# Attention with a hashed mask and two gated mixers on one core: the first pair of heads is read from one buffer and prepared by three engines

## The chip, the cores and the metric

The program runs on 1 core of a Trainium2 chip. The metric is device time in microseconds of one execution, as the median of several. Before the change it is 559.13 us (three runs, 557.96 to 561.72).

## What is computed

The reference has three stages: attention under a mask made from hashes, then two gated mixers on its output. The changed code belongs to the first stage alone.

```
def _attn_ref(q, k, v, proj):                     # 2 batches, 8 heads, 768 rows, 64 columns
    q_bits = (q @ proj > 0); k_bits = (k @ proj > 0)          # 6 bits for each row
    mask = q_bucket[:, :, :, None] == k_bucket[:, :, None, :]
    scores = np.where(mask, scale * q @ k^T, -1e9)
    attn = softmax(scores)
    return attn @ v
x = moe(attn)        # k = relu(xk @ w_k); sigmoid(xr @ w_r) * (k*k @ w_v)
return moe2(x)       # two projections, normalised rows, a product over the sequence
```

All values are float32. The kernel gets that accuracy on TensorE from rounded values: a number is split into a rounded part and a low part (x minus the rounded part), and products of both are summed.

## The kernel before

**Tiling.** Heads come in 8 pairs (`pp`). A pair has two heads, `e` = 0 and 1. Its queries are cut into two halves of 384, and each half gives six units: for each head three blocks (`j`) of 128 queries against all 768 keys. So there are 96 units. The loop `for p in range(np3)` handles three units in each of its 32 iterations, p = 0 to 31.

**A unit.** `scores` (L326) makes 128 x 768 scores in PSUM with four matmuls over 128 rows. The operand of a head is `tk` (`TK[pp % 2][e]`, 128 x 4 x 768): slots 0 and 3 are the rounded k and q, slot 1 holds the low part of k in one half of the rows and the hash bits of k in the other, and slot 2 the rounded q and the hash bits of q. Thus the mask is part of the same matmuls, with bits scaled by 2^30. `peak` (L336, VectorE) copies the scores out of PSUM and takes each row's maximum, `bias` (L344, VectorE) scales it, `expo` (L354, ScalarE) takes the exponential and the sum, `move` transposes six blocks on TensorE (L364) and copies them to `PT` (L370, ScalarE), and `av` (L399, TensorE) multiplies by v. The first `av` comes in iteration 3, for the units of iterations 0 and 1. Buffers limit how far engines run apart: `s` has two, `p` three, `t` (PSUM) three, `PT` two.

**Preparing a pair.** `load_x` fetches x, the pair's k and q (768 KB). `load_pair` fetches the same rows again with four transfers of POOL's queue that round on the way, straight into slots 0 and 2 of one half of the rows and slots 0 and 3 of the other. `split_part` or `split_piece` subtracts to get the low parts. `bits_mm` (L275) multiplies x with the hash vectors, `bits_sign` (L282) and `bits_scale` (L289) make scaled bits of them, and `bits_place` puts eight strips of 12 x 384 into the two `tk`. For the first pair all this stands ahead of the loop: two strips each on VectorE (L303) and ScalarE (L305), four by SP's queue (L307). `clear` (L311) sets the rows beside the bits to zero.

**Warming.** `warm(n)` issues n matmuls of the identity (L267), whose results nobody reads: 12 at the very start, 8 behind the first bits.

**The order of the work.** The order is written out by hand. Each engine does its instructions in program order. The dictionary `plan` keeps further work at slots (p, k): k = 0 behind the second exponential of iteration p, k = 1 at its end. Under it stand the next pair's loads and splits, and the weights of the later stages, 512 x 128 in a unit (`weight_jobs`): a load by SP's queue, `magnitude` on ScalarE (L41), `clamp` (L44), `shift` (L49), `top` (L55), `power` (L62), `low` (L65) on VectorE, `first` on ScalarE (L71), `rest` on POOL (L76, L77). `plan_unit` puts the steps of a unit around an iteration `p0`, by one of the tables `late`, `soon` and `first`.

## Time and profile before

| what | value |
|---|---|
| median of three runs | 559.13 us |
| the profiled execution's own time | 557.71 us |
| its span, from the first to the last instruction | 555.9 us |
| busy TensorE | 543.1 us (98%) |
| busy VectorE, ScalarE, POOL | 370.6, 335.6, 144.6 us |
| mean granted TensorE clock | 0.997 |
| chain that ended last, by engine | PE 86%, DVE 7%, ACT 5%, issue 1%, DMA 1% |

PE is TensorE, DVE is VectorE, ACT is ScalarE, SP is the engine whose queue issues most loads. The profiled execution was 1.42 us faster than the median, and 1.81 us of its time lie outside the span.

### The profile page before, as it was taken

The page shows a single profiled execution, that of the slowest core. Times are in us where ns is not written, and L with a number is a line of the kernel's source. Part 1 is how long each engine was busy: PE and PEld are TensorE (multiplying, and loading weights), DVE is VectorE, ACT ScalarE, POOL GpSimd, SP SyncE. Part 2 cuts the span into 40 slices and gives each one's busy share as a digit, 9 for nine tenths or more (in the row PEclk, how much of TensorE's full clock was granted, in tenths as well). Part 3 has the DMA queues.
Part 4 walks back from the last instruction along what each step waited for, and adds up shares of the span by engine and source line. Part 5 has one row for each costly group of instructions (what it writes and reads, how often), then busy time and mean ns, then how long its engine had stood idle before and what let it go on. Part 6 is the DMA issues. An engine that isn't in the chain of part 4 may idle for free.

```text
span 555.9 us, 9001 instructions
## 1 busy us (share of the span) xinstructions
PE 543.1 (98%) x3188; PEld 466.4 (84%) x3188; DVE 370.6 (67%) x812; ACT 335.6 (60%) x718; POOL 144.6 (26%) x152
## 2 busy tenths in 40 slices
PE   7899999999999999999999999999999999999997
PEld 6766767676767677689999999999998999899896
DVE  6688787877877779458796775316997784443230
ACT  1888888888888889749843856429345343221211
POOL 5684948485857533200000000000110000000000
PEclk9899999999999999999999999999999999999999
DMA  8949494949595710210031211000572100001102
GB/s 175 270 142 177 127 190 125 194 135 181 143 173 168 151 49 16 72 71 26 15 113 39 73 42 39 0 1 8 191 228 85 58 29 1 2 19 39 57 20 95
DMA packets 20478, 51.96 MB, mean 93 GB/s; under 512 B 3841, under 2 KB 6865, under 8 KB 20433
## 3 DMA queue, kind: packets, MB, share of 16 engines
q1 hardware_dynamic: 13664, 31.44, 18.4%
q0 software_dynamic: 6336, 19.66, 17.7%
q8 instruction: 25, 0.41, 0.3%
q10 hardware_dynamic: 432, 0.28, 0.2%
q14 instruction: 21, 0.16, 0.1%
HBM read 47.08 MB, written 3.19 MB: 90 GB/s over the span
## 4 chain that ended last, share of the span: by engine, by line
PE 86%; DVE 7%; ACT 5%; issue 1%; DMA 1%; ACTq 0%; DVEq 0%; POOLq 0%
PE s L326 11%; PE o L399 11%; PE t L364 11%; PE o L176 11%; PE v L638 9%; PE k L176 8%; PE s L176 7%; PE w L176 5%; PE u L176 5%; PE o L638 3%; PE r L176 3%; DVE p L336 2%; DMA tk<-in_kq_dram 1%; ACT tk L121 1%; ACT p L354 1%
## 5 line engine op out<-in xcount | busy, mean ns | idle before, releaser
L336 DVE TENSOR_SCALAR_CACHE_REDUCE p<-s 128x768 f32<-128x768 f32 x96 | 91.8, 956 | 29.4 <-PE s L326 27.9
L354 ACT ACTIVATE p<-p,nb 128x768 f32<-128x768 f32 x96 | 90.5, 943 | 14.0 <-DVE nb L344 13.2
L370 ACT COPY PT<-t 128x384 f32<-128x384 f32 x192 | 83.6, 477 | 19.9 <-PE t L364 18.8
L326 PE MATMUL s<-tk 128*128 128x384 f32 x384 | 85.0, 355 | 3.8 <-DVE p L336 2.1
L326 PEld LDWEIGHTS s<-tk 128*128 128x128 f32 x384 | 64.6, 190 | 23.1 <-DVE rt L382 6.6
L364 PE MATMUL t<-ident,p 128*128 128x128 f32 x576 | 80.4, 280 | 3.4 <-ACT p L354 1.7
L364 PEld LDWEIGHTS t<-ident,p 128*128 128x128 f32 x576 | 65.5, 142 | 14.6 <-ACT PT L370 5.0
L399 PE MATMUL o<-PT,v 128*64 128x384 f32 x384 | 68.8, 494 | 0.0
L258 POOL TENSOR_TENSOR tk<-x,tk 64x384 fp32r<-64x384 f32 x56 | 59.1, 1086 | 2.5 <-issue 1.6
L176 PE MATMUL k<-tk,wk 128*128 128x384 f32 x336 | 59.6, 334 | 0.0
L176 PEld LDWEIGHTS k<-tk,wk 128*128 128x128 f32 x336 | 58.4, 188 | 0.0
L638 PE MATMUL v<-k,wv 128*128 128x384 f32 x288 | 53.6, 334 | 0.0
L638 PEld LDWEIGHTS v<-k,wv 128*128 128x128 f32 x288 | 50.3, 188 | 0.0
L399 PEld LDWEIGHTS o<-PT,v 128*64 128x64 f32 x384 | 24.8, 136 | 28.5 <-issue 26.5
L697 POOL DMA_DIRECT2D wsp<-in_w_spT_dram x6 | 3.6, 612 | 167.8 <-DVE w_a L44 161.3
L176 PE MATMUL o<-wk,tk 128*128 128x512 f32 (+1 forms) x168 | 36.2, 374 | 0.0
L176 PEld LDWEIGHTS o<-wk,tk 128*128 128x128 f32 x168 | 30.0, 188 | 5.5
L619 ACT ACTIVATE kr<-k 128x384 f32<-128x384 f32 x28 | 13.6, 487 | 31.2 <-PE k L176 31.0
L176 PE MATMUL r<-tk,wr 128*128 128x384 f32 x168 | 30.9, 338 | 0.2 <-DVE tk L122 0.2
L121 ACT CAST tk<-g 128x384 fp32r<-128x384 f32 x16 | 8.2, 514 | 37.5 <-DVE g L768 37.5
L176 PE MATMUL w<-wk,tk 128*128 128x512 f32 x132 | 30.7, 390 | 0.0
L176 PEld LDWEIGHTS r<-tk,wr 128*128 128x128 f32 x168 | 29.1, 188 | 1.9 <-ACT PT L370 0.6
(108 smaller groups left out, 851.1 us busy)
## 6 DMA issues: line engine op xcount, KB each, us to landing
tk<-in_kq_dram POOLq DMA_DIRECT2D x32, 384.0 KB, 9.7
x<-in_kq_dram POOLq DMA_DIRECT2D x6, 768.0 KB, 5.6
w_raw<-in_w_k_dram SPq DMA_DIRECT2D x8, 512.0 KB
w_raw<-in_w_v_dram SPq DMA_DIRECT2D x8, 512.0 KB
w_raw<-in_w_in_dram SPq DMA_DIRECT2D x8, 512.0 KB
v<-in_vP_dram SPq DMA_DIRECT2D x8, 384.0 KB
rb<-ds SPq DMA_DIRECT2D x32, 96.0 KB
out_dram<-ot SPq DMA_DIRECT2D x11, 256.0 KB
```

What stands on the lines that cost most here:

```text
L121: nc.scalar.copy(hi, src)
L176: nc.tensor.matmul(o, a, x, start=(i == 0), stop=(i == len(seq) - 1))
L258: nc.gpsimd.tensor_sub(tk[l, 1 + 2 * t, o], raw[pp][l, t, o], tk[l, 2 * t, o])
L326: nc.tensor.matmul(s[:, c, :HS], w, t[:, n, c * HS:(c + 1) * HS], start=(n == 0), stop=(n == 1),)
L336: nc.vector.tensor_scalar(c, s[:, :, :HS], -BIG / 2, None, op0=ALU.max, op1=ALU.max, accum_out=m)
L354: nc.scalar.activation(c, c, AF.Exp, bias=nb, scale=0.125, accum_out=den[g][:, u:u + 1])
L364: nc.tensor.transpose(t[:, 128 * n:128 * n + 128], p[:, k0:k0 + 128], ident)
L370: nc.scalar.copy(PT[g][:, e, 3 * c:3 * c + 3, 128 * j:128 * j + 128], t[:, :HS].rearrange("p (n q) -> p n q", n=3),)
L399: nc.tensor.matmul(obank[64 * e:64 * e + 64, :HS], vt[g // 2][:, kt, e, :], PT[g][:, e, kt, :], start=(kt == 0), stop=(kt == 5),)
L619: nc.scalar.activation(r, o[:, :HS], AF.Relu)
L638: nc.tensor.matmul(os[m][:, :HS], w, x, start=(c == 0 and k == 0), stop=(c == 7 and k == 2),)
L697: nc.gpsimd.dma_start(wsp[c // 3][:, 0, c % 3, :], w_spT[128 * c:128 * c + 128, :])
```

## The change

The first pair is prepared in another way, the second pair's loads and the first weights are moved ahead, and one evacuation is moved.

- Loads at the start: x of the first pair comes in two transfers, k first and then q, into a `PT` buffer (`load_halves`). SP's queue then fetches x of the second pair (its buffer `x` is free for that), the first weight unit and v. POOL's queue fetches only head 1's `tk` (two transfers in place of four).
- Head 0's `tk` is made from x by copies: on VectorE (k, one half of the rows), ScalarE (k, the other half; q) and POOL (half of q). The subtractions are on VectorE (k of both heads) and POOL (q, in halves, `first_low`).
- Bits: `bits_mm` runs twice, the second time with the hash vectors shifted by 12 columns (`msc` gets two columns for that), so that each head's strips lie on rows where an engine can take them. `place` scales and writes a strip in one instruction: two on VectorE, four on ScalarE, two on POOL. `bits_scale` and the four transfers of L307 are gone for this pair.
- `make_identity` moves to the start, `warm` gets 7 and 3 matmuls in place of 12 and 8, and the 3 stand behind the scores of units 0 and 1. Zero fills are shared by VectorE and POOL, all four at the start.
- POOL issues the second pair's four transfers in the middle of the first pair's preparation, behind a subtraction that needs head 1's data.
- The subtraction of head 1's k (VectorE) moves into slot (0, 0).
- The first weight unit follows a new table `start`: `magnitude` in (0, 1), `clamp` and `shift` in (1, 0), `top` in (2, 0), `first` and `power` in (2, 1), one iteration or half of one earlier than by `first`.
- The last evacuation of iteration 0 is VectorE's.

```diff
-WARM_A, WARM_B = 12, 8
+WARM_A, WARM_B = 7, 3
+        def load_halves(pp):
+            b, p = divmod(pp, NP)
+            raw[pp] = mid.tile([128, 2, S], F32, tag="PT", bufs=2, name="x")
+            for t in range(2):
+                nc.sync.dma_start(raw[pp][:, t, :], kq[b, p, t])
...
+        def place(zb, e, g, eng):
+            dst, src, by = place_at(0, e, g), zb[32 * g:32 * g + 12, :], cst_sb[32 * g:32 * g + 12, 1:2]
+            if eng is nc.scalar:
+                nc.scalar.mul(dst, src, by)
+            else:
+                eng.tensor_scalar(dst, src, by, None, op0=ALU.mult)
+
+        def first_low(e, n):
+            l, o = lo_rows[e], slice(n * HS, n * HS + HS)
+            t = TK[0][e]
+            nc.gpsimd.tensor_sub(t[l, 3, o], raw[0][l, 1, o], t[l, 2, o])
+
+        def first_pair():
+            x, t = raw[0], TK[0][0]
+            lo, hi = lo_rows[0], hi_rows[0]
+            h0, h1 = slice(0, HS), slice(HS, S)
+            nc.vector.tensor_copy(t[lo, 0, :], x[lo, 0])
+            nc.scalar.copy(t[hi, 0, :], x[lo, 0])
+            nc.vector.tensor_sub(t[lo, 1, :], x[lo, 0], t[lo, 0, :])
+            nc.scalar.copy(t[lo, 2, h0], x[lo, 1, h0])
+            nc.scalar.copy(t[hi, 3, h0], x[lo, 1, h0])
+            nc.scalar.copy(t[lo, 2, h1], x[lo, 1, h1])
+            first_low(0, 0)
+            nc.gpsimd.tensor_copy(t[hi, 3, h1], x[lo, 1, h1])
+            bits_mm(0)
+            bits_sign(0)
+            z0 = zs.pop(0)
+            place(z0, 0, 2, nc.vector)
+            place(z0, 0, 3, nc.scalar)
+            place(z0, 0, 0, nc.vector)
+            bits_mm(0, 12)
+            bits_sign(0, "zc")
+            z1 = zs.pop(0)
+            for g in (2, 3, 0):
+                place(z1, 1, g, nc.scalar)
+            first_low(1, 0)
+            load_pair(1)
+            first_low(0, 1)
+            place(z0, 0, 1, nc.gpsimd)
+            place(z1, 1, 1, nc.gpsimd)
+            first_low(1, 1)
...
+        start = ((-2, 1), (-1, 0), (-1, 0), (0, 0), (0, 1), (0, 1), (1, 0), (1, 0))
...
-            plan_unit(2 + 2 * n, late if n % 2 else soon if n else first, ld, jobs)
+            plan_unit(2 + 2 * n, late if n % 2 else soon if n else start, ld, jobs)
...
         nc.scalar.dma_start(msc, misc)
-        nc.vector.memset(ident, 0.0)
-        load_x(0)
-        load_pair(0)
-        clear(0, nc.vector)
+        load_halves(0)
+        make_identity(nc, ident)
+        load_pair(0, (1,))
+        clear(0, 0, nc.vector)
+        clear(1, 0, nc.vector)
+        clear(0, 1, nc.gpsimd)
+        clear(1, 1, nc.gpsimd)
+        load_x(1)
+        for job in plan.pop((-1, 1)):
+            job()
+        load_v(0)
         warm(WARM_A)
-        split_part(0, 0, 1, nc.gpsimd)
-        split_part(0, 0, 0, nc.vector)
-        bits_mm(0)
-        bits_sign(0)
-        bits_scale(0, nc.vector)
-        bits_place(0, True)
-        warm(WARM_B)
+        first_pair()
         for r in rcs:
             nc.vector.memset(r, 0.0)
-        split_part(0, 1, 0, nc.vector)
-        split_part(0, 1, 1, nc.gpsimd)
-        make_identity(nc, ident)
-        load_v(0)
+        plan.setdefault((0, 0), []).insert(0, lambda: split_part(0, 1, 0, nc.vector))
...
-            move(a + 1, 1)
+            move(a + 1, 1, nc.scalar.copy if p else nc.vector.tensor_copy)
```

VectorE at the start of the program, before the change, from its first instruction to the first unit's maximum (`tk_0_77` is head 0's operand, `tk_1_78` head 1's):

```order
L489 MEMSET ident 128x128
L311 MEMSET tk_0_77 64x1536
L311 MEMSET tk_1_78 64x1536
L263 TENSOR_TENSOR tk_0_77<-x,tk_0_77 64x768
L282 TENSOR_SCALAR zb<-z,msc 128x384
L289 TENSOR_SCALAR zc<-zb,msc 128x384
L303 CAST tk_0_77<-zc 12x384 x2
L502 MEMSET rc_89 128x32
L502 MEMSET rc_90 128x32
L263 TENSOR_TENSOR tk_1_78<-x,tk_1_78 64x768
L336 TENSOR_SCALAR p,m<-s 128x768
```

The same stretch of VectorE in the change, from behind its two zero fills (the maximum of a unit is L379 there):

```order
L327 CAST tk_0_77<-x 64x768
L329 TENSOR_TENSOR tk_0_77<-x,tk_0_77 64x768
L288 TENSOR_SCALAR zb<-z,msc 128x384
L316 TENSOR_SCALAR tk_0_77<-zb,msc 12x384 x2
L288 TENSOR_SCALAR zb<-z,msc 128x384
L548 MEMSET rc_89 128x32
L548 MEMSET rc_90 128x32
L379 TENSOR_SCALAR p,m<-s 128x768
L387 TENSOR_SCALAR nb<-m 128x1
L379 TENSOR_SCALAR p,m<-s 128x768
L387 TENSOR_SCALAR nb<-m 128x1
L269 TENSOR_TENSOR tk_1_78<-x,tk_1_78 64x768
```

Head 1's subtraction (last row) went from ahead of the first maximum to behind the second one, the separate scaling is gone, and a copy and a second sign have come in.

POOL at the start of the program in the change, from its first transfers on (`tk_0_87` and `tk_1_88` are the second pair's operands):

```order
L252 DMA tk_1_78<-in_kq_dram 64x2x768
L253 DMA tk_1_78<-in_kq_dram 64x2x768
L354 MEMSET tk_1_78 64x1536
L354 MEMSET tk_1_88 64x1536
L321 TENSOR_TENSOR tk_0_77<-x,tk_0_77 64x384
L334 CAST tk_0_77<-x 64x384
L321 TENSOR_TENSOR tk_1_78<-x,tk_1_78 64x384
L252 DMA tk_0_87<-in_kq_dram 64x2x768
L253 DMA tk_0_87<-in_kq_dram 64x2x768
L252 DMA tk_1_88<-in_kq_dram 64x2x768
L253 DMA tk_1_88<-in_kq_dram 64x2x768
L321 TENSOR_TENSOR tk_0_77<-x,tk_0_77 64x384
```

Before, POOL issued four transfers for the first pair, did two subtractions of 64 x 768, made the identity and filled with zeros, and only then issued the second pair's four; now these stand behind the third of its short operations, and two strips and another subtraction follow them.

VectorE in iteration 2, before the change, from the second maximum to the third:

```order
L336 TENSOR_SCALAR p,m<-s 128x768
L344 TENSOR_SCALAR nb<-m 128x1
L379 TENSOR_SCALAR rc_89<-den 128x6
L380 RECIPROCAL rc_89<-rc_89 128x6
L382 STREAM_TRANSPOSE rt<-rc_89 128x32
L44 TENSOR_SCALAR w_a<-w_a 128x512
L49 TENSOR_SCALAR w_a<-w_a 128x512
L336 TENSOR_SCALAR p,m<-s 128x768
```

In the change these two weight steps stand one iteration earlier, ahead of the second pair's sign:

```order
L379 TENSOR_SCALAR p,m<-s 128x768
L387 TENSOR_SCALAR nb<-m 128x1
L44 TENSOR_SCALAR w_a<-w_a 128x512
L49 TENSOR_SCALAR w_a<-w_a 128x512
L288 TENSOR_SCALAR zb<-z,msc 128x384
L379 TENSOR_SCALAR p,m<-s 128x768
```

Behind the reciprocals of iteration 2 stands `top` (L55) alone.

## Rows read from the trace of the kernel before

**Rows 1.** Busy time by stretch (start:end length, PE, PEld, DVE, ACT, POOL, clock, DMA share, GB/s)

```profile
0.00:33.40 33.40, 26.67 (x156) 21.91 (x157) 23.50 (x50) 17.84 (x39) 22.11 (x30) 0.95 0.87 192
33.40:330.00 296.60, 294.38 (x1836) 233.54 (x1836) 228.83 (x535) 232.51 (x507) 118.81 (x117) 1.00 0.46 113
```

**Rows 2.** Chain that ended last, 0 to 40 us (start us, us, what)

```profile
1.24 6.28 DMA tk<-in_kq_dram
...
8.53 0.63 DVE zb L282
...
9.19 1.21 DVE zc L289
...
10.42 0.35 DVE tk L303
...
11.24 2.57 DVE tk L263
13.81 0.89 DVE p L336 x2
...
14.91 1.04 ACT p L354 x2
...
28.39 0.76 DVE w_a L44
...
29.16 1.10 DVE w_a L49
...
33.41 2.09 PE o L399 x12
```

**Rows 3.** Timeline of VectorE and POOL at the first subtractions (start us, us, engine line op)

```profile
7.55 0.95 DVE L263 TENSOR_TENSOR tk<-x,tk 64x768 fp32r<-64x768 f32 x1 [3.25 <-DMA tk<-in_kq_dram]
7.60 2.57 POOL L263 TENSOR_TENSOR tk<-x,tk 64x768 fp32r<-64x768 f32 x1 [3.79 <-DMA tk<-in_kq_dram]
...
11.18 1.83 POOL L263 TENSOR_TENSOR tk<-x,tk 64x768 fp32r<-64x768 f32 x1 [1.01 <-DVE tk L303]
```

**Rows 4.** Timeline of TensorE up to the first scores

```profile
1.05 5.39 PE L267 MATMUL o<-ident 128*128 128x128 f32 x24 [1.05 <-DVE ident L489]
...
6.38 0.85 PE L275 MATMUL z<-x,msc 128*32 128x384 f32 x8
...
7.16 2.05 PE L267 MATMUL o<-ident 128*128 128x128 f32 x16
```

**Rows 5.** Timeline of ScalarE, 10 to 33 us (in brackets idle time before, and its releaser)

```profile
10.42 1.03 ACT L305 CAST tk<-zc 12x384 fp32r<-12x384 f32 x2 [7.92 <-DVE zc L289]
...
18.61 0.85 ACT L370 COPY PT<-t 128x384 f32<-128x384 f32 x2
21.01 0.48 ACT L370 COPY PT<-t 128x384 f32<-128x384 f32 x1 [1.55 <-PE t L364]
...
31.42 0.94 ACT L354 ACTIVATE p<-p,nb 128x768 f32<-128x768 f32 x1 [1.37 <-DVE nb L344]
```

**Rows 6.** Busy time in single microseconds (columns as in rows 1)

```profile
13.00:14.00 1.00, 0.00 (x0) 0.00 (x0) 1.00 (x2) 0.00 (x0) 0.93 (x5) 1.00 0.09 18
...
18.00:19.00 1.00, 1.00 (x5) 1.00 (x4) 0.00 (x0) 1.00 (x4) 1.00 (x3) 0.50 1.04 412
```

**Rows 7.** DMA queue of SP from 4 to 5 us (packets, MB, share of 16 engines)

```profile
q1 hardware_dynamic: 84, 0.21, 52.3%
```

**Rows 8.** Transfers of POOL's line L246, from issue to landing

```profile
DMA to landing us min/median/max: 6.3/9.3/11.3
```

**Rows 9.** Groups by line and form, 0 to 200 us (count, busy us, mean ns, idle us before)

```profile
L336 DVE TENSOR_SCALAR_CACHE_REDUCE p<-s 128x768 f32<-128x768 f32 x83 | 79.4, 956 | 26.8 <-PE s L326 25.3 <-ACT p L354 1.2
...
L258 POOL TENSOR_TENSOR tk<-x,tk 64x384 fp32r<-64x384 f32 x56 | 59.1, 1086 | 2.5 <-issue 1.6
L246 POOL DMA_DIRECT2D tk<-in_kq_dram x16 | 10.0, 626 | 0.8 <-POOLq L871 0.8
L311 POOL MEMSET tk<- 64x1536 f32 x2 | 2.7, 1374 | 0.1
```

More of the change, by code (lines that the diff above doesn't have):

```diff
@@ L109, in hash_attention_moe_kernel @@
     ident = per.tile([128, 128], F32, name="ident")
-    msc = per.tile([128, 42], F32, name="msc")
+    msc = per.tile([128, 44], F32, name="msc")
     pb, cst_sb = msc[:, 0:32], msc[:, 32:34]
@@ L239, in load_x, with load_pair @@
             (nc.gpsimd if pp > 1 else nc.sync).dma_start(raw[pp], kq[b, p].rearrange("t r s -> r t s"))
-        def load_pair(pp):
+        def load_halves(pp):
             b, p = divmod(pp, NP)
-            for e in range(2):
+            raw[pp] = mid.tile([128, 2, S], F32, tag="PT", bufs=2, name="x")
+            for t in range(2):
+                nc.sync.dma_start(raw[pp][:, t, :], kq[b, p, t])
+        def load_pair(pp, es=(0, 1)):
+            b, p = divmod(pp, NP)
+            for e in es:
                 src = kq[b, p][:, 64 * (1 - e):64 * (1 - e) + 64].rearrange("t d s -> d t s")
@@ L269, in attention, with bits_mm @@
         zs = {}
-        def bits_mm(pp):
+        def bits_mm(pp, c0=0):
             zs[pp] = ps_t.tile([128, 512], F32, tag="t", name="z")
@@ L275, in bits_mm, with bits_sign @@
                 nc.tensor.matmul(
-                    zs[pp][32 * g:32 * g + 32, :HS], pb, raw[pp][:, 1 - g // 2, o:o + HS],
-                    start=True, stop=True,
-                )
-        def bits_sign(pp):
-            zb = at.tile([128, HS], F32, tag="zb", name="zb")
+                    zs[pp][32 * g:32 * g + 32, :HS], msc[:, c0:c0 + 32],
+                    raw[pp][:, 1 - g // 2, o:o + HS], start=True, stop=True,
+                )
+        def bits_sign(pp, tag="zb"):
+            zb = at.tile([128, HS], F32, tag=tag, name="zb")
             nc.vector.tensor_scalar(
@@ L290, in bits_scale, with place_at, bits_place @@
             zs[pp] = zc
-        def bits_place(pp, first=False):
+        def place_at(pp, e, g):
+            o = (g % 2) * HS
+            return TK[pp % 2][e][64 * e:64 * e + 12, 2 - g // 2, o:o + HS]
+        def bits_place(pp):
             zc = zs.pop(pp)
@@ L295, in bits_place @@
                 for g in range(4):
-                    o = (g % 2) * HS
-                    a0 = 64 * e
                     s0 = 32 * g + 12 * e
-                    dst = TK[pp % 2][e][a0:a0 + 12, 2 - g // 2, o:o + HS]
-                    src = zc[s0:s0 + 12, :].bitcast(F32)
-                    if first and e == 0:
-                        if g % 2:
-                            nc.vector.tensor_copy(dst, src)
-                        else:
-                            nc.scalar.copy(dst, src)
-                    else:
-                        nc.sync.dma_start(dst.bitcast(F32), src)
@@ L309, in clear @@
-        def clear(r, eng):
-            for e in range(2):
-                eng.memset(TK[r][e][hi_rows[e], 1:3, :].bitcast(F32), 0.0)
+                    nc.sync.dma_start(
+                        place_at(pp, e, g).bitcast(F32), zc[s0:s0 + 12, :].bitcast(F32)
+                    )
+        def place(zb, e, g, eng):
[4 more added lines that the diff above has]
+                eng.tensor_scalar(dst, src, by, None, op0=ALU.mult)
@@ L313, in attention, with clear @@
+        def clear(r, e, eng):
+            eng.memset(TK[r][e][hi_rows[e], 1:3, :].bitcast(F32), 0.0)
         nunits = npairs * 12
@@ L365, in transp, with evac @@
             return t
-        def evac(i, c, t):
+        def evac(i, c, t, copy=nc.scalar.copy):
             g, u = divmod(i, 6)
             e, j = divmod(u, 3)
-            nc.scalar.copy(
+            copy(
                 PT[g][:, e, 3 * c:3 * c + 3, 128 * j:128 * j + 128],
@@ L451, in attention @@
         first = ((-1, 1), (0, 0), (0, 0), (1, 0), (1, 0), (1, 0), (1, 1), (1, 1))
+        start = ((-2, 1), (-1, 0), (-1, 0), (0, 0), (0, 1), (0, 1), (1, 0), (1, 0))
         def plan_unit(p0, where, ld, jobs, keys=range(8)):
-            at_slot(max(p0 - 3, 0), 1, ld)
+            at_slot(p0 - 3, 1, ld)
             for k in keys:
@@ L476, in attention @@
             if pp >= 0:
-                at_slot(p0, 0, lambda n=pp + 1: load_pair(n))
+                if pp:
+                    at_slot(p0, 0, lambda n=pp + 1: load_pair(n))
                 at_slot(p0 + 1, 0, lambda n=pp + 1: bits_mm(n))
@@ L509, in attention @@
         nc.gpsimd.tensor_scalar(omu, msc[:, 34:42], -1.0, 1.0, op0=ALU.mult, op1=ALU.add)
-        clear(1, nc.gpsimd)
         def av3(p):
@@ L514, in av3, with move @@
                 av(p // 2, 3 * (p % 2) + n)
-        def move(i, c):
-            evac(i, c, transp(i, c))
+        def move(i, c, copy=nc.scalar.copy):
+            evac(i, c, transp(i, c), copy)
         def score(i):
@@ L526, in attention @@
             scores(a + 1)
+            if not p:
+                warm(WARM_B)
             score(a)
@@ L828, in _misc @@
 def _misc(proj, mu_k, mu_r):
-    c = np.zeros((128, 42), np.float32)
+    c = np.zeros((128, 44), np.float32)
     for o in range(2):
```

4 lines of the change are left out of this document (2 added, 2 removed).

## The prediction

> **What bounds the kernel now.** The table of busy time by stretch comes first, since it says where an edit at the start can count at all [rows 1]. From 33.4 to 330 us TensorE is busy for 294.38 of 296.6 us, and up to 33.4 us for 26.67 of 33.4. So behind 33.4 us work follows on TensorE without a gap, and whatever lets the first multiplication with v start earlier moves all that follows by as much. That instruction starts at 33.41 [rows 2]. The prediction is therefore about one number: when does it start after the change.
>
> The chain of waits says what leads to it [rows 2]. POOL's transfer for head 0 lands at 7.5 us (issued at 1.24, 6.28 us). Then VectorE subtracts, signs (8.53), scales (9.19, for 1.21 us), places a strip (10.42, 0.35 each), subtracts for head 1 (11.24, for 2.57 us), and only then takes the first maximum, in the chain at 13.81. The first exponential starts at 14.91. From there to 33.41 ScalarE is the engine to look at: its timeline has only two long gaps, 1.55 us before 21.01, where it waited for transposes, and 1.37 us before 31.42, where it waited for a maximum [rows 5]. The first lies behind the stretch in which the granted clock is 0.50, that is 1.2 GHz in place of 2.4; TensorE had been idle for the whole of the 14th microsecond before that [rows 6]. The second lies behind `clamp` and `shift` on VectorE (28.39 and 29.16), which stand ahead of a maximum [rows 2].
>
> So of the 33.4 us some 14.9 are preparation, and 16.5 (14.91 to 31.42, the ninth exponential) are ScalarE's row of work with 2.92 us of gaps. The ninth exponential releases the transposes that stand just ahead of the first multiplication with v.
>
> **Two waits inside the preparation.** The timeline of the two engines shows a further one [rows 3]. VectorE's subtraction at 7.55 takes 0.95 us; POOL's, of the same size and begun 0.05 later, takes 2.57 and ends at 10.17. VectorE's scaling, begun at 9.19, ends at 10.40, 0.2 behind it. At 11.18 POOL is first (1.83 us, to 13.01), and this time VectorE's subtraction takes 2.57 us, to 13.81: 0.8 after POOL's end. Whoever comes second stands still until the other's instruction has ended. This costs VectorE about 1.0 us in the scaling and 1.6 us in head 1's subtraction, both on the chain.
>
> **Arrival of x, and the bits.** x is 768 KB; its last packets on SP's queue move between 4 and 5 us, 0.21 MB in that microsecond [rows 7], and its first reader starts at 6.38, directly behind a warming matmul [rows 4]. So x can be read somewhere from 5.0 to 6.4; I take 6.0, nearer the reader, since completion needs time behind the last packet. The same bytes in two transfers arrive at the same time, k's half about 1 us ahead (0.39 MB at the rate of rows 7, with the fewer packets of the other queue). Head 0 no longer waits for POOL's transfer, which landed at 7.5.
>
> The bits take TensorE 0.85 us [rows 4]: 6.85. Whether at that speed depends on the clock: the 24 warming passes took 5.39 us, 0.22 each, the 16 later ones 2.05, 0.13 each, so the first ones ran at the lower level. In the change TensorE begins later (the identity comes from POOL), with 14 passes instead of 24, and waits for x. At the lower level the two sets of bits would take 3.4 instead of 1.7 us. I take the fast one for the sum and keep the other for the range.
>
> Sign on VectorE: 0.63 [rows 2]. Ahead of it on VectorE stand the rounding copy of k and the subtraction: 64 x 768 elements, between 0.35 (a strip, rows 2) and 0.95 for the copy, for which I take 0.6, and 0.95 for the other. With k there at 5.0 they end at 6.55. But POOL now fills two buffers with zeros at that time, 1.37 each [rows 9], behind two transfers of 0.63 each; if a fill holds up the copy as the subtractions hold up each other, copy and subtraction end at some 7.55. In between: sign from 7.3 to 7.95. Two strips on VectorE, 0.35 each, with up to 1.1 us of waiting for POOL's subtraction of 64 x 384 [rows 9], for which I take 0.5: 9.15. ScalarE's three copies of 64 x 384 cost about 0.5 each (12 x 384 took 0.51 each [rows 5]) and its strip comes in beside VectorE's. Scores of the first unit end at 9.6 (half of them need no bits), the second sign and two small fills at 9.9, and the first maximum begins there, against 13.81 in the chain: 3.9 us earlier, at best 4.8 and at worst 2.8.
>
> The Trainium skill speaks against this change on one point. Its page "SBUF — State Buffer", section "SBUF: two separate sides", says that VectorE and POOL share a pair of ports as an exclusive lock, held for a whole instruction, and that fast one-source copies in SBUF need it. Rows 3 agree. By that rule the rounding copy and both strips are all candidates, and the sign would begin at 7.55 and the strips end at 9.8, which is 0.65 us less gain than the sum has; by the rows, which show no zero fill beside such a copy, between nothing and that.
>
> **The first exponential.** ScalarE now places three strips of head 1 between the second sign (9.8) and it: three times 0.51 [rows 5], 11.35. The maximum and the scaling behind it take 1.1 (13.81 to 14.91, rows 2), so their result is there at 11.0 and ScalarE is the later one: 11.35 against 14.91, 3.55 us earlier.
>
> **From there to the ninth exponential.** ScalarE's row of work is unchanged but for one evacuation less, 0.4 (0.85 for two, rows 5). 16.51 less 1.55, 1.37 and 0.4 is 13.2 us. The 1.55 goes if the clock stays up: the idle time ahead of the drop came from head 1's subtraction, and that wait is gone. The 1.37 goes because of `clamp` and `shift` leaving iteration 2; the `top` that remains is one step instead of three. Two new waits come in. In iteration 0 head 1's subtraction (0.95) now stands ahead of the third maximum: 9.9 plus three maxima at 1.1 and 0.95 is 14.15, and ScalarE wants the third at 11.35 + 2.8 = 14.15 (by the order of its work, two exponentials and two evacuations at the paces of rows 5). That fits exactly, so each lock is a stall: I take 0.3, bounds 0 and 1.1. In iteration 1 `clamp` and `shift` now precede the sixth maximum, with 0.76 and 1.10 [rows 2] (with waits for POOL in them), while ScalarE gets there about 8 us behind its first exponential; VectorE was held for 1.2 us in iteration 2's first maximum by the `p` buffers [rows 9], so a part is slack. I take 0.9, bounds 0 and 1.9. ScalarE's `magnitude` (L41) moves only within the row.
>
> So the ninth exponential starts at 11.35 + 13.2 + 0.3 + 0.9 = 25.75 against 31.42: 5.65 earlier. For the chance of some half-speed matmuls and other small waits I take off 0.35: **5.3 us**. The loads cost nothing in this sum: x of the second pair, v and the first weights are wanted after 15 us, and head 1's two transfers, issued at 2 to 3 us, land by 9.3 us later, 12 [rows 8], against some 13.6 for its first scores. The edit of the zero fills and of the identity costs nothing, since x is not there before.
>
> The profiled execution took 557.71 us; 557.71 - 5.3 = 552.4. The median of the runs is 1.42 us above it, so the median after should be **553.8 us**. A difference of 1% (5.6 us) is about what a measurement of this kernel can tell from none.
>
> **Rivals.**
> 1. *The whole sum.* No lock is hit, the clock stays up: first exponential at 10.5, no new stall. Then the ninth comes at 23.7 to 24.6, and 6.8 us are won: 552.3 or less. For it: the rows show locks only between operations that happen to meet. Against: the change gives VectorE and POOL more such operations.
> 2. *The clock.* TensorE is short of work before x and between bits and scores, runs the bits and first scores at the lower level (0.85 to 1.7 us), and falls again as at 16 to 20 us (1.55, rows 5). Then some 3 us remain: 556.1. For it: fewer warming passes, and rows 6 show the drop after an idle microsecond. Against: the transposes start earlier, so the gaps are shorter.
> 3. *Head 1 is late.* Its two transfers have to share with 1.7 MB of SP's queue that now stands behind x. At the longest landing, 11.3 us after issue at 2.7 [rows 8], they come at 14; the subtractions of both engines wait, the third maximum comes at some 16 and a further 2 us are lost: 3.3 us won, 555.8. A rule of the Trainium skill bears on it: "DMA: Bandwidth & Descriptors", section "Queues, rings and completion order", says that each engine takes turns between queues packet by packet. By that POOL's transfers are slowed, but not kept waiting for all of SP's; no row here shows 1.7 MB standing ahead of them.
> 4. *Slower.* POOL's instructions are in order, and behind its wait for head 1 stand four issues (2.5 us), two subtractions (2.2) and two strips (up to 1.1 each), at whose end the units of iteration 2 and 3 may start: 7 to 8 us behind the landing. If head 1 landed only after about 20 us, the scores of iteration 3 would come at 27 to 28 us, two to three us late for the sum above and with the stalls of iterations 1 and 2 ahead of them, so that the gain would be gone; from there on the kernel is slower by as much as the landing is late: at 22 us some 1 to 2 us, 560. Rows 8 with 11.3 at the most make that unlikely.
>
> **Chances.** The forecast (4 to 6.3 us) 0.47, rival 1 0.2, rival 2 0.15, rival 3 0.13, rival 4 0.05. Faster by over 1% means over 5.6 us: rival 1 and somewhat under half of the forecast, 0.4. Slower 0.05, the rest, within 1%, 0.55. The range goes from 551.5 (rival 1 with its bound) to 556.6 (rivals 2 and 3 at their prices).
>
> **What will show it.** In the profile after: the first maximum at 9 to 11 us; the first exponential right behind ScalarE's strips, at 10.5 to 12; no stretch of clock 0.50 from 13 to 20 us; a gap of ScalarE ahead of the sixth exponential of up to 1 us, none ahead of the ninth; the first multiplication with v at 27 to 29 us; behind it the same times as before, moved. I am wrong if TensorE has new gaps behind that point, if the clock falls, or if VectorE's copy or strips stand longer than 1.5 us.

## The result, and the profile after

The changed kernel took **552.07 us** (median of 4 runs, 551.32 to 552.56). The kernel before, run beside it, took 558.68 (557.96 to 561.72). The ratio is 0.987, with a 95% interval of 0.9831 to 0.9909. The difference of 6.6 us flatters the change. Later on the change was run twice more: 551.77 beside 557.37 (0.9892, 0.9873 to 0.9911) and 552.45 beside 557.65 (0.9905, 0.9891 to 0.992). Over all runs taken, the median of before is 557.74 (73 runs) and that of the change 552.09 (15 runs): **5.65 us, 1.01%**. That it is faster is shown: each of the three intervals lies below 1. Whether by more than 1%, the prediction's bound between faster and the same, is open.

The page of the changed kernel, its first part and its chain by engine, with an execution of 552.09 us:

```profile
span 550.3 us, 8974 instructions
...
PE 538.5 (98%) x3176; PEld 462.1 (84%) x3176; DVE 373.8 (68%) x813; ACT 339.4 (62%) x723; POOL 145.8 (26%) x155
...
PE 86%; DVE 7%; ACT 5%; issue 1%; ACTq 0%; DVEq 0%
```

Busy time by stretch after (columns as in rows 1), cut at the new start of the first multiplication with v:

```profile
0.00:28.80 28.80, 22.32 (x144) 17.40 (x144) 25.45 (x50) 21.17 (x44) 23.97 (x33) 1.00 0.80 193
28.80:325.40 296.60, 294.38 (x1838) 234.00 (x1838) 230.38 (x536) 232.90 (x507) 118.21 (x117) 1.00 0.46 113
```

The second line repeats that of [rows 1]: TensorE is busy for 294.38 of 296.6 us in both kernels. The change lies in the first stretch. There VectorE is now busy for 25.45 of 28.8 us (23.50 of 33.4 before).

The chain of waits after, which answers to [rows 2] (start, length, what):

```profile
4.08 1.87 DVE tk L327
...
7.65 0.63 DVE zb L288
...
9.13 0.53 DVE zb L288
...
11.00 0.61 ACT tk L314
...
11.64 1.04 ACT p L397 x2
...
15.39 0.98 DVE p L379 x2
...
17.65 1.09 DVE w_a L44
...
19.11 0.61 DVE zb L288
...
23.47 0.75 DVE rc L422
...
24.68 1.02 DVE w_b L55
...
26.85 1.04 ACT p L397 x2
...
28.85 2.09 PE o L442 x12
```

Read the first and the last line that matter: the multiplication with v starts at 28.85 instead of 33.41, **4.56 us earlier**. Between 15.39 and 26.77 the chain is VectorE's, but for some 1.4 us of ScalarE behind 20.88.

Where the 5.65 us come from can be counted along TensorE. The shift is 4.56 at the first multiplication with v, and 4.82 at the last one of the program (551.77 to 546.95). The other 0.8 is at the very end. The last packet of the output was written at 553.87 before and at 549.03 after, but the span ends at 555.9 and 550.3, which is 2.0 and 1.3 behind it. SP closes the program with nine waits on semaphores. Three of them are for the output's transfers. The records show that in before one other wait and these three come first, and five more are taken one by one behind the last of the three, from 554.36 to 554.96. After the change all six others come first, from 545.43 to 545.74, while the output is still being computed, and the three stand last. The waits of SP's queue show the end of this, in before and after (longest 1.6 and 1.3 us):

```profile
SPq L880 <- DMA out_dram<-ot: 3.9, 3, 1.6
```

```profile
SPq L924 <- DMA out_dram<-ot: 3.5, 3, 1.3
```

All kernels made from before end 4.1 us behind the start of the last matmul, and all made from the change 3.3 to 3.5, whatever they do at the start. No line of the diff asks for this, and what decides the order of these waits was not tried.

### The profile page after: what moved, and what is told of

Read it like the earlier page. It is cut to its first block, busy times and chain, and to the rows that moved or that the text cites. A ratio compares the mean times of both kernels' runs of the same rounds, so it can differ in the third digit from the quotient of the medians.

```text
span 550.3 us, 8974 instructions
## 1 busy us (share of the span) xinstructions
PE 538.5 (98%) x3176; PEld 462.1 (84%) x3176; DVE 373.8 (68%) x813; ACT 339.4 (62%) x723; POOL 145.8 (26%) x155
## 4 chain that ended last, share of the span: by engine, by line
PE 86%; DVE 7%; ACT 5%; issue 1%; ACTq 0%; DVEq 0%
PE o L442 11%; PE o L176 11%; PE s L369 11%; PE t L407 11%; PE v L682 9%; PE k L176 8%; PE s L176 7%; PE w L176 5%; PE u L176 5%; PE o L682 3%; PE r L176 3%; DVE p L379 2%; ACT tk L121 1%; PE z L281 1%; DVE tk L122 1%
## 5 line engine op out<-in xcount | busy, mean ns | idle before, releaser
L379 DVE TENSOR_SCALAR_CACHE_REDUCE p<-s 128x768 f32<-128x768 f32 x96 | 91.7, 956 | 24.4 <-PE s L369 24.1
L369 PEld LDWEIGHTS s<-tk 128*128 128x128 f32 x384 | 63.9, 188 | 21.1 <-DVE w_a L44 6.7
```

Of the source, the lines that this page charges most:

```text
L369: nc.tensor.matmul(s[:, c, :HS], w, t[:, n, c * HS:(c + 1) * HS], start=(n == 0), stop=(n == 1),)
L379: nc.vector.tensor_scalar(c, s[:, :, :HS], -BIG / 2, None, op0=ALU.max, op1=ALU.max, accum_out=m)
```

## Experiments

What is compared is the time, and from each trace the start of the first, sixth and ninth exponential and of the first multiplication with v (14.91, 24.35, 31.42 and 33.34 in before; 11.64, 20.88, 26.85 and 28.78 in the change, each from the first record of its kind).

### Head 1's subtraction alone

The kernel before with one edit of the change (run b_split_late):

```diff
-        split_part(0, 1, 0, nc.vector)
+        plan.setdefault((0, 0), []).insert(0, lambda: split_part(0, 1, 0, nc.vector))
```

> The kernel before, with one part of the change alone: head 1's subtraction on VectorE moved from ahead of the first maximum into iteration 0 behind the second one. Theory: its 2.57 us (1.6 of them a wait for POOL) leave the chain, the first maximum starts at 12.2 to 12.4 instead of 13.74, TensorE's idle time from 12.8 to 14.7 shrinks and the clock does not fall; the first multiplication with v comes 1.5 to 3 us earlier than 33.4. Rival: the second and third maximum and ScalarE's row take it back; then it comes within 0.7 us of 33.4.

Measured: 557.21 us, ratio 0.9996 (0.9982 to 1.0009). The first exponential came at 13.24, 1.7 us earlier; the ninth at 31.55, no earlier. The timeline says where the gain went:

```profile
20.49 0.98 PE L275 MATMUL z<-x,msc 128*32 128x384 f32 x8 [2.12 <-DMA x<-in_kq_dram]
...
21.52 0.62 DVE L282 TENSOR_SCALAR zb<-z,msc 128x384 f32<-128x384 f32 x1 [2.13 <-PE z L275]
...
23.73 0.48 ACT L370 COPY PT<-t 128x384 f32<-128x384 f32 x1 [2.95 <-PE t L364]
```

The bits of the second pair wait 2.12 us for its x, and VectorE and ScalarE wait behind them. The start was shorter, and the next thing that was late ate it: a transfer that before had been hidden. The edit itself had a part in that: the second pair's x goes into the buffer that the moved subtraction reads, so its load was issued at 15.28, and at 14.36 in before. From 21.1 to 24.5 the granted clock was 0.50 as well.

### The second pair's x late again

The change with that transfer taken from the start and issued by ScalarE's queue, at 12.08 (14.36 in before; run a_x1late2):

```diff
-        load_x(1)
+        plan.setdefault((0, 0), []).append(lambda: load_x(1, nc.scalar))
```

> The change with one transfer put back near its old time: the second pair's x is issued by ScalarE behind the first exponentials (about 13.5 us; 14.36 in the kernel before) and not at the start. Theory 'the early x is a needed part of the change': the bits of the second pair wait for x by some 2 us, its sign and the rows behind it come later, the ninth exponential is 1.5 to 2.5 us later than the change's 26.85, time 553 to 554.5. Rival 'the transfer is hidden in either place', as the prediction's sum has it: ninth exponential within 0.4 us of 26.85, time within 0.5 us of the change's.

Measured: 557.43 us (554.22 to 561.07), ratio 0.9992 (0.9969 to 1.0015). **The whole gain is gone**, more than either theory gave. The transfer shares the DMA engines with the second pair's four transfers on POOL's queue, issued from 11.35 to 13.77:

```profile
12.08 9.91 DMA x<-in_kq_dram
...
22.13 1.51 PE z L281 x8
```

```profile
22.13 1.51 PE L281 MATMUL z<-x,msc 128*32 128x384 f32 x8 [5.52 <-DMA x<-in_kq_dram]
...
25.64 0.86 ACT L413 COPY PT<-t 128x384 f32<-128x384 f32 x2 [6.62 <-PE t L407]
```

It lands 9.9 us after its issue. TensorE idles for 5.52 us, the granted clock is 0.50 from 21.8 to 25.2, and the ninth exponential starts at 32.60. The early load is a condition of the gain in this order of the transfers. Of the places tried for it, here and in two runs below, none gave a lower median than where it now stands.

### Head 0 from POOL's rounding transfers again

The change without the copies of head 0 (L327, L328, L330 to L332, L334), and with `load_pair(0)` for both heads (run a_poolhead0).

> The change, with head 0's rounded k and q again by two rounding transfers of POOL's queue instead of copies from x. Theory: the copies from x are the main part of the gain, since POOL's transfers land at 7.5 us at the earliest (as before) and later beside SP's traffic; the first maximum comes at 11.5 to 13 instead of 9.84 us, head 1's data 2 to 4 us later too, and the kernel loses 2 to 4 us of the gain. Rival: the reordering (locks, clock, weights) made the gain; then the loss is under 1 us.

Measured: 558.59 us, ratio 1.0017 (1.0006 to 1.0027). Again nothing is left, where the expectation had a loss of 2 to 4 us. Beside SP's loads, head 0 lands far later than the 7.5 us of [rows 2]. Its first transfer is used at 11.72, and the scores wait for the second, in the chain until 14.77:

```profile
11.72 0.95 DVE L327 TENSOR_TENSOR tk<-x,tk 64x768 fp32r<-64x768 f32 x1 [7.67 <-DMA tk<-in_kq_dram]
```

```profile
2.15 12.62 DMA tk<-in_kq_dram
...
14.90 2.92 PE s L363 x8
```

The granted clock was 0.50 from 8.7 to 19.0 us, so a part of the loss is the first scores at that level. Without the copies the early loads gain nothing, and without the early x the copies gain nothing: each needs the other here.

### Head 1's subtraction ahead of the first maximum again

The change with `split_part(0, 1, 0, nc.vector)` back in its old place (run a_split_early).

> The change with VectorE's subtraction for head 1 put back where it stood, ahead of the first maximum. Theory of the prediction: then the first maximum waits for head 1's transfers, which land at some 11.2 us, and for the subtraction of 0.9 behind them: first maximum at 12.2 or later (9.84 in the change), first exponential 2.2 or more later; what is left of that at the ninth exponential is 0.5 to 2 us, time 552.5 to 554. Rival 'the stretch 15 to 27 us is bound by VectorE whatever stands first': the subtraction costs the same there as here, the ninth exponential within 0.4 us of 26.85 and time within 0.5 us of the change's.

Measured: 553.74 us, ratio 0.9939 (0.992 to 0.9958), some 1.6 us of the gain lost.

```profile
10.81 0.95 DVE L269 TENSOR_TENSOR tk<-x,tk 64x768 fp32r<-64x768 f32 x1 [1.07 <-DMA tk<-in_kq_dram]
```

VectorE waits 1.07 us for head 1 and needs 0.95: the first maximum is at 11.69 instead of 9.84, the first exponential 1.22 later and the ninth 1.44 later (28.29). What the start loses, the ninth exponential loses too. The rival, that the stretch behind hides it, falls.

### The old table for the first weights

> The change, with the first weight unit at the old table's places (clamp and shift in iteration 2, top in iteration 3). By the prediction's sum the move was worth 1.37 less 0.9, so undoing it costs 0.5 us: ScalarE's gap ahead of the sixth exponential (1.10 us now) goes and one of 1.4 to 2 us stands ahead of the ninth (0.85 now). Rival: VectorE is the full engine from 15 to 27 us, and with top out of that stretch it has 1.1 us less to do before the ninth maximum; then the first multiplication with v comes 0.5 to 1 us earlier than 28.8 and the kernel is that much faster, unless iteration 3 gives it back.

`start` replaced by `first` in `plan_unit` (run a_first): 552.37 us, ratio 0.9905 (0.989 to 0.9921). The profiled execution got off to a better start (first exponential at 10.33) and yet reached the ninth only at 26.65, with a gap of 1.05 us of ScalarE there. Between the two it took 16.3 us, where the change took 15.2. Of these 1.1 us, 0.53 are a wait ahead of the third exponential, for head 1's data, which the change's trace does not have; so what is left for the new table is some 0.6 us, by this pair of traces. The time does not show it: the multiplication with v came at 28.57, a little before the change's 28.78, because of the start, and the next experiments are about that.

### POOL's zero fill at the port

The copy at 4.08 took 1.87 us in the chain; in a_first it took 0.56. What POOL does beside it in the change:

```profile
2.83 2.69 POOL L354 MEMSET tk<- 64x1536 f32 x2
...
4.08 1.85 DVE L327 CAST tk<-x 64x768 fp32r<-64x768 f32 x1
...
5.97 1.65 DVE L329 TENSOR_TENSOR tk<-x,tk 64x768 fp32r<-64x768 f32 x1
```

The fills end at 5.52, and the copy 0.41 behind them; the subtraction is held in the same way by POOL's subtraction from 5.64 to 6.80. In the first trial (a_fill_late) the second fill goes behind POOL's copy in `first_pair`:

```diff
+            clear(1, 1, nc.gpsimd)
...
-        clear(1, 1, nc.gpsimd)
```

> The change, with POOL's zero fill for the second pair moved from ahead of its first subtraction to behind its first copy. Theory 'ports': VectorE's rounding copy of k took 1.85 us (4.08 to 5.93) because POOL's two zero fills ran until 5.52 and held it up; with one fill less it ends at 5.1 or before, the first maximum starts at 8.5 to 9 instead of 9.84 us, and the kernel gains 0.8 to 1.4 us on the change. Rival: a rounding copy of 64 x 768 takes that long by itself; then it stays at 1.8 us, and the time is the same within 0.3 us.

Measured: 552.18 us, ratio 0.9902 (0.9886 to 0.9917); no gain. The copy is short now, but the fill holds the two strips instead:

```profile
4.08 0.56 DVE L327 CAST tk<-x 64x768 fp32r<-64x768 f32 x1
...
7.30 1.37 POOL L355 MEMSET tk<- 64x1536 f32 x1
...
7.43 1.87 DVE L316 TENSOR_SCALAR tk<-zb,msc 12x384 fp32r<-12x384 f32 x2
```

In the second trial (a_fill_end) it goes behind `load_pair(1)`, where VectorE has no short copies:

> The change, with POOL's zero fill for the second pair moved to behind the second pair's four transfers, where VectorE has no copy or strip waiting. Theory 'ports, then head 1': the rounding copy takes 0.56 us from 4.08, the two strips 0.8 to 1.3 without the wait of 1 us that the fill caused in the run before (1.87), and the first maximum starts at 8.3 to 9 instead of 9.84 us; but then head 1's two transfers bind (they came at 11.5 and 14.0 us in the run in which the start happened to be fast), and the ninth exponential gains only 0.2 to 0.6 on 26.85; the kernel is 0.1 to 0.6 us faster than the change. Rival: only the start of the first exponential counts; then the ninth gains the same 1 to 1.4 us.

Measured: **550.95 us**, ratio 0.9892 (0.9873 to 0.9912), the lowest median of all kernels. The copy takes 0.56, the strips 1.12, the first exponential starts at 10.23 and the multiplication with v at 27.77, 1.0 earlier than in the change. The ninth exponential starts at 25.44, 1.41 earlier, which is the number of the rival and not the 0.2 to 0.6 of the theory. In between, the lead of 1.4 us at the first exponential shrinks to 0.4 at the sixth:

```profile
20.45 0.94 ACT L398 ACTIVATE p<-p,nb 128x768 f32<-128x768 f32 x1 [1.55 <-DVE nb L388]
```

The chain ahead of it is POOL's. The second pair's sign goes into the buffer `zb`, which POOL's first strip still has to read, and POOL's moved fill stands ahead of that strip:

```profile
14.78 1.37 POOL tk L355
...
17.34 1.31 POOL tk L316
...
18.68 0.62 DVE zb L288
...
20.45 1.03 ACT p L398 x2
```

So the late fill spared VectorE a wait at the start, and then stood in the way of POOL's strip. That this kernel beats the change is not shown: its median lies 1.1 us under that of all runs of the change (552.09), but the ratio, taken beside other runs of before, is the 0.9892 that the change had once too, and two of its six runs took 552.3 and 552.4.

### Other places for the loads

First x of the second pair on POOL's queue behind head 1, and v behind the second pair, on top of the late fill (a_best); then x and the first weights issued by ScalarE between the rows of the two heads, the second weights and v later still, and the fill behind POOL's last subtraction (a_best2).

> The same, and x of the second pair and v go to POOL's queue, behind head 1's transfers, so that SP's queue has 1.0 MB of weights instead of 2.2 MB behind x. Theory 'ports, then head 1': head 1 lands at 9 to 10.5 and 11 to 12 us, no wait for it is left, the first exponential starts at 10.3 and the ninth at 25.4 to 26; the kernel is 0.8 to 1.4 us faster than the change (550.4 to 551 beside 551.8). Rival: the share of the two queues does not matter (POOL's transfers are slow by themselves, 0.2 MB in a microsecond), head 1 lands as before, and the kernel is within 0.4 us of the run with the fill alone.

> The change with POOL's last zero fill behind its last subtraction of the first pair, the second pair's x and first weights issued by ScalarE between the rows of the two heads (about 7.3 us), the second weights one unit later and v behind the second pair's sign rows. Theory 'the stretch 15 to 27 us is bound by VectorE, and what POOL does at the port sets its length': ninth exponential at or under 25.4 (26.85 in the change, 25.44 with the fill behind the load of the second pair), first v multiplication 27.7 or earlier, time 550 to 551. Rival 'the queues set it': head 1 lands sooner than in the change because SP's queue is empty beside it, but x of the second pair lands later and the second pair's bits wait for it; then the ninth exponential comes at 26.5 or later and the time is 552 or more.

Measured: 552.56 (0.9917, 0.9899 to 0.9935) and 553.43 (0.9926, 0.9908 to 0.9944). Both medians lie above that of the late fill alone. A line of each shows what became late, the second pair's x in the first and v in the second (in the first, head 1's scores had waited 1.49 for its transfer as well, at 14.60):

```profile
18.30 0.85 PE L281 MATMUL z<-x,msc 128*32 128x384 f32 x8 [1.42 <-DMA x<-in_kq_dram]
```

```profile
30.37 0.87 PE L446 MATMUL o<-PT,v 128*64 128x384 f32 x4 [1.77 <-DMA v<-in_vP_dram]
```

### Is the stretch from 15 to 27 us bound by VectorE?

The change with the first weight unit's steps moved later (run c_w_late; its clamp, shift and upper half stand behind the ninth maximum), beside the change itself on the same chip (a_again):

```diff
-        start = ((-2, 1), (-1, 0), (-1, 0), (0, 0), (0, 1), (0, 1), (1, 0), (1, 0))
+        start = ((-1, 1), (0, 1), (0, 1), (1, 0), (1, 0), (1, 0), (1, 1), (1, 1))
```

> The change with the first weight unit's work after its load moved later by about an iteration, so that VectorE's clamp, shift and upper half (1.17, 0.43 and 1.09 us in the change) stand behind the ninth maximum. Theory 'the stretch from the third to the ninth maximum is bound by VectorE': sixth exponential 1.2 to 1.6 us earlier than in the change (19.4, and without the gap of 1.10), ninth exponential 24.2 to 25 (26.85 in the change), time 550 or less if the work is not paid again later. Rival 'something else, TensorE's and ScalarE's row or the sign rows, is right behind': ninth exponential 26.2 or later, time within 0.5 us of the change's.

> The change itself, beside the two kernels of this batch on the same chip: 551.5 to 552.5, ratio 0.988 to 0.991.

Measured: 551.43 us (0.9887, 0.987 to 0.9905), and the change 552.45. The sixth exponential starts at 19.73 and the ninth at 25.64, 1.15 and 1.21 earlier than in the first trace of the change, from the same start (11.71); beside a_again's trace it is 1.11 and 1.55. By the times alone the gain is not shown, since the two intervals overlap. ScalarE's two waits in the change, and the same two exponentials in c_w_late, without a wait:

```profile
20.88 0.94 ACT L397 ACTIVATE p<-p,nb 128x768 f32<-128x768 f32 x1 [1.10 <-DVE nb L387]
...
26.85 0.94 ACT L397 ACTIVATE p<-p,nb 128x768 f32<-128x768 f32 x1 [0.85 <-DVE nb L387]
```

```profile
19.73 0.94 ACT L397 ACTIVATE p<-p,nb 128x768 f32<-128x768 f32 x1
...
25.64 0.94 ACT L397 ACTIVATE p<-p,nb 128x768 f32<-128x768 f32 x1
```

In the chain VectorE has disappeared from this stretch:

```profile
14.62 1.39 PE s L369 x8
...
20.43 1.39 PE s L369 x8
...
25.86 1.39 PE s L369 x8
...
27.90 2.08 PE o L442 x12
```

VectorE did bound it, as the theory says, but 2.7 us of its work bought 1.2, and 0.95 at the multiplication with v. The rival was half right: the row of TensorE and ScalarE is 1.2 us behind.

> Both edits: POOL's last zero fill behind the load of the second pair, and the first weight unit's work later. Theory 'VectorE bounds both stretches, one after the other': the gains add up, ninth exponential 23 to 23.8 (25.44 with the fill alone), first v multiplication 25.4 to 26.2, time 548.5 to 549.8. Rival 'head 1's landing or the second pair's rows are next': a wait for the transfers or for the second pair's scores takes what VectorE gives back, first v multiplication 27 or later, time 550.5 or more.

With the late fill as well (c_both): 552.21 us (0.9905, 0.9888 to 0.9921). The gains do not add up. In the profiled execution, more than half of the start's gain was missing (first exponential at 11.04, not 10.23), with the bits at about half the pace (16 matmuls in 2.79 us, not 1.50, though the profile's clock reads 1.00 there); and from 15 us on its chain is that of the kernel above, with the multiplication with v at 27.96. Its time is that of the rival, but neither of the two things that the rival named, a wait for the transfers or for the second pair's scores, shows in its chain. Off the chain, VectorE's sign for the second pair again waited for POOL's strip, 0.78 us, and the sixth exponential 0.44.

### The clock

> The change as it is, once more, to see how much of the difference of the medians (6.6 us) is the kernel's. In the two traces TensorE's last group of matmuls (535.58 before, 530.76 after) moved by 4.8 us, the output's last transfer ended 0.8 us sooner behind it, and the profiled execution of before lay 1 us under its median. If only the 4.8 us are the kernel's doing, the medians differ by 4.5 to 5.8 us here; if the end or something outside the trace belongs to it, by 6.3 to 7.

The change again (run a_same): 551.77 us, 5.60 less than before. By its number this is the first case of the expectation; but the 1 us by which the profiled execution of before lay under its median did not come back, and the last 0.8 us are the kernel's by the traces, since every kernel made from the change ends in that way. This time the granted clock was 0.51 in the stretch in which the scores start:

```profile
9.20:12.70 3.50, 3.50 (x13) 3.50 (x14) 2.89 (x10) 2.90 (x6) 1.70 (x3) 0.51 1.18 262
```

Six score matmuls took 2.21 us (1.31 in the first trace), and the multiplication with v came 0.3 later, at 29.10. That is not the clock's doing as far as is shown: the first exponential came at 11.63, as in the first trace, and in a_again, with the clock at 1.00 throughout, the multiplication came at 29.11. Then all warming matmuls were taken out (`WARM_A, WARM_B = 0, 0`; run a_cold):

> The change without any warming matmuls. Theory 'warming buys only the clock of the first scores, and the stretch behind them is bound by VectorE': z and the first score groups at the granted clock 0.50, the first exponential 0.3 to 1.2 us later, the ninth less than 0.6 us later, time 551.8 to 552.8. Rival 'the clock sets the start': every score group before 15 us costs 0.9 more (2.21 for six instead of 1.31), the ninth exponential 1.5 us or more later, time 553.5 or more.

Measured: 552.19 us, ratio 0.9904 (0.9884 to 0.9923); no loss.

```profile
4.98 2.79 PE L281 MATMUL z<-x,msc 128*32 128x384 f32 x16 [4.98 <-DMA x<-in_kq_dram]
...
9.18 3.72 PE L369 MATMUL s<-tk 128*128 128x384 f32 x10 [0.47 <-DVE tk L316]
```

The bits take 1.3 us longer and the scores 0.37 us each, as in the stretch at 0.51 above. The profile's clock reads 1.00 there, so that only the durations tell the lower level. VectorE was not free to read the bits before (its subtraction ends at 7.61), and the first exponential waits for ScalarE's strips: 11.63, as in the change. In this start the slower matmuls are hidden.

Last, the kernel before with warming between its first scores (run b_warm). The kernel that ran had 12 warming instructions there, not the 5 its expectation speaks of:

> The kernel before, with five warming matmuls more, behind the scores of units 0 and 1, where TensorE is idle. It tells what the fall of the clock (0.50 from 16.5 to 19.9 us) costs by itself. Theory: the clock stays up, the gap of 1.55 us in ScalarE's timeline goes, and the first multiplication with v comes 1 to 1.6 us earlier than 33.4. Rival: the gap is a wait for VectorE's side anyway; then under 0.5 us.

Measured: 558.92 us, ratio 1.0027 (1.0011 to 1.0043). The clock stayed at 1.00, and the multiplication with v still came at 33.88. But the warming itself waited for the identity until 14.44, took 2.94 us and pushed scores back, so what the fall in before costs stays open. Another thing differed: with the same code up to there, VectorE's subtraction for head 1 was now ahead of POOL's (0.95 us at 11.24, not 2.57), and the first exponential came at 13.34. So the wait of 1.6 us that the prediction read in [rows 3] need not be in every execution of before.

## Why the prediction was right or wrong

The range held the time (552.07 in 551.5 to 556.6), but the likeliest class, within 1%, did not come. The forecast of 5.3 us stood below that bound; 6.6 us were measured in the first runs, and 5.65 over all runs stand on it. Two steps of the sum failed, in opposite directions: up to the ninth exponential the gain was put 1.08 us too high, because VectorE's waits were priced too low, and the end of the program was put at nothing, where 0.8 us came. The time fell into the range by luck in part, since these errors and the added offset partly cancel, and 552.07 is the number of rival 1 without its mechanism: a lock was hit and two waits came. One of the prediction's own signs of being wrong came true, too: VectorE's copy stood 1.85 us, over 1.5. By steps:

- **Bound and place: right.** One number, the start of the first multiplication with v, carried through: 4.56 us there, 4.82 at the last matmul.
- **First maximum: right in the sum (9.84 for 9.9), by errors that cancel.** k's half of x was readable at about 4.05, not 5.0. The copy took 1.85 us instead of 0.6, and the subtraction 1.65 instead of 0.95. The Trainium skill, page "SBUF — State Buffer", section "SBUF: two separate sides", has the lock that explains it; the trace agrees, with 1.85 us beside the fill and 0.56 without. That case was priced in the prediction from the zero fill: the sign at 7.55 by the rule, 7.3 in the sum. It began at 7.65.
- **First exponential: 0.29 late** (11.64 for 11.35). The three strips took 1.86 us in all and not 1.53.
- **To the ninth exponential: the first step that failed.** "The 1.37 goes because of clamp and shift leaving iteration 2" is not what happened: 0.85 of that gap stayed. In iteration 0 no stall came (0.3 allowed), and the sixth exponential waited 1.10 (0.9). Together 15.21 us instead of 14.4. The sum treated the stretch as ScalarE's row with two gaps, each closed by its own edit. ScalarE's row itself was right (13.26 us without the two gaps, 13.2 in the sum). But VectorE had almost no slack from 15.39 on (busy for 9.53 of 10.23 us up to the ninth maximum), so moving `clamp` and `shift` forward within the stretch moved a good part of the wait and did not remove it. c_w_late, which takes them and `top` out of it, removes both gaps; in exchange ScalarE waits 0.68 for transposes, at 16.38. How the wait is shared out changes from trace to trace: in a_fill_end, with the table of the change, the sixth exponential waits 1.55 and the ninth not at all, for the same 15.21 us. There the first step of the reciprocals (L423) took 0.16 us (0.23 in before), and in the change (L422) 0.82; why is not shown. Beside the 5.65 us that the sum gave at the ninth exponential, 4.57 were measured.
- **"The loads cost nothing in this sum": true, and misleading.** x of the second pair was treated as neutral; b_split_late and a_x1late2 show that without its early start nothing is gained. A sum that walks one chain prices a part at zero when the part only keeps the next chain from taking over.
- **The margin of 0.35** for the clock and small waits was not needed for the clock (1.00 throughout), but more than that was lost in the two gaps. The warming passes at the two paces (0.22 and 0.13 us each) that the prediction read as two levels have a clock of 1.00 in the profile, so the level is told there from the durations alone.
- **The end: the second step that failed, 0.8 us that the sum did not have.** "Behind it the same times as before, moved" did not hold: the span ends 3.3 us behind the start of the last matmul and not 4.1. By the records that is the order of SP's closing waits; what sets the order stays open.
- **The offset.** 1.42 us were added because the profiled execution lay below the median of three runs. Over 73 runs the median is 557.74, that of the profiled execution (557.71). The first runs of before lay high: 558.68 is 0.97 over the profiled execution, and these 0.97 make 6.6 out of a gain of 5.62 between the two profiled executions. Of the 1.7 us between forecast and result 1.4 are this offset. The gain itself was missed by 0.35: 1.1 too much up to the ninth exponential, 0.35 taken off, 0.25 more along the attention and 0.8 at the end.
- **Rivals.** The clock (2) fell early in a_same, and no loss from that is shown there. Head 1 (3, 4) was not late: POOL took it up at 10.26. What rival 4 has of POOL's order did come, as a small wait: in a_fill_end POOL's strip held the second pair's sign. In four microseconds, 5 to 9, POOL's queue moved 0.86 MB when it was alone, in before, and after the change 0.50 beside SP's 0.76:

```profile
q0 software_dynamic: 312, 0.86, 132.0%
```

```profile
q1 hardware_dynamic: 246, 0.76, 71.6%
q0 software_dynamic: 177, 0.50, 44.2%
```

So it is slowed but not kept waiting. That is what the Trainium skill's page "DMA: Bandwidth & Descriptors", section "Queues, rings and completion order", has of the packet-wise turns. What rival 3 feared came true in a_poolhead0, where twice the bytes stood on that queue: POOL took head 1 up at 18.19.

## What to carry to other kernels

Where several chains lie within a microsecond or two of each other, put each part of a change back alone: here three of them were worth 1.6 us (the subtraction), 5.3 (the early x) and 6.5 (the copies), which add up to more than twice the gain, and the one that was also tried alone on the old kernel was worth nothing there. When a gap is to be closed, ask whether the engine that made it has slack anywhere in the stretch: if it has little, an operation must leave the stretch, since moving it within mostly moves the gap. And take the level of a forecast from all the times at hand, with little weight on where one profiled execution lies among three runs.

## What the runs showed of the hardware that was not expected

- A zero fill of 64 x 1536 by POOL holds up a copy by VectorE: 1.85 us instead of 0.56 for 64 x 768. Who comes first was not the same in every run of like code: in seven traces of kernels with both fills ahead the copy took 1.85, and in the eighth, a_first, it won at the same 4.08 and took 0.56 (the two fills then took 3.12). In all five with a fill moved away it took 0.56.
- SP's closing waits, 0.8 us, as told above.
- A load of 768 KB that shares with four transfers of 384 KB of another queue took 9.9 us. The runs of that kernel spread over 7 us (554.22 to 561.07), where most spread over 0.5 to 2; that the load's time varied is the likely reason, but it is not shown, since one execution was traced.
